# Attention and two-matrix MoE on one core: twelve chunks of GELU on VectorE, and last units of two chunks

## The chip, the core and the metric

The kernel runs on one core of a Trainium2 chip. The metric is the device time of one execution in microseconds (us). The core has a matmul engine (TensorE, PE in the profile; its weight loads are PEld), a vector engine (VectorE, DVE), an engine for activation functions (ScalarE, ACT), GpSimd (POOL) and SyncE (SP), which here only issues DMAs. Each engine works through its own instructions in order and waits for others by semaphores.

## What is computed

```python
kv_pool = kv.reshape(B, H // 4, 4, W // 4, 4, C).mean(axis=(2, 4))
k = v = kv_pool.reshape(B, -1, C) @ w_sr          # 768 keys of 128 per batch
s = (q @ k.transpose(0, 2, 1)) / np.sqrt(C)       # softmax over the keys
x = (softmax(s) @ v).reshape(B * N, C)            # 49152 rows of 128
h = x @ w_in                                      # 128 -> 2048
out = (h / (1 + np.exp(-1.702 * h))) @ w_out      # 2048 -> 128
```

B is 4, N 12288, C 128. The last line is a GELU in its sigmoid form.

## The kernel before

**Tiles and stages.** The rows are cut into 96 groups of 512. For a group the attention has 6 chunks (128 keys x 512 rows of scores, one exponential each) and the MoE 16 chunks (128 of the 2048 hidden columns x 512 rows, one GELU each). There are two rounds of 48 groups: attention, MoE, attention, MoE. The second MoE, groups 48 to 95, is the last stage.

**Units.** ScalarE takes mostly three chunks at a time, a unit of 128x1536 from three banks of PSUM; units alternate between banks 0 to 2 and 3 to 5. TensorE fills a unit with three matmuls (`fill_attn`, L330; `fill_moe`, L513), ScalarE writes exp or GELU of it to a frame of `ag` in SBUF (L332, L515), and TensorE drains each chunk later: four matmuls of 128x129 with v for attention (L341), one of 128x512 with w_out for the MoE (`drain_moe`, L523). A group's 16 drains sum up in one accumulator bank, 6 or 7; then VectorE transposes it out of PSUM (L531) and SP issues four DMAs to the output. Groups use the two banks in turn. The very last group is drained in small matmuls of 128x128 (`drain_last`, L544) into banks 2, 5, 6 and 7, the one that the group before still holds last; VectorE and ScalarE copy the result out, half each.

**Chunks of exponentials on VectorE.** 32 attention chunks do not go through ScalarE: 24 of four "early" groups and 8 "rolling" ones (`early_fill`, `early_exp`). TensorE makes their scores in one of the two accumulator banks (L373); VectorE reads them there in its first step (L389) and then computes 2 to the power of z by splitting off the integer part as exponent bits (L391 to L395) and a polynomial of degree five (L397, L400, L402). The steps are dealt out one by one between VectorE's other work. The rolling ones are kept in `aside`, three places of their own.

**What sets the order.** The order on every engine is fixed when the program is written, by a planner at the end of the kernel. Its clock counts in matmuls of 512 columns. It holds estimates of when TensorE (`now`), VectorE (`dve`) and each unit of ScalarE (`end`) will be done, with

```python
FIXED, CHUNK, SWITCH, HANDOVER, EVACUATE = 0.295, 1.978, 6.0, 1.0, 4.5
end.append(begin + FIXED + CHUNK * len(part))
limit = end[-1] - K - HANDOVER if n + 3 < len(seq) else 1e9
```

For each unit n it places the fills of unit n + 2, and then drains as long as they end before `limit`, so that the next fills are in time for ScalarE. A unit of three counts 6.229 of these units on ScalarE, and three fills and three drains count 6 on TensorE, so that now and then a fourth drain fits. Chunks that ScalarE has made and TensorE has not drained wait in `ag` (102 places); they are the backlog. `seq` is the list of units. In the second MoE it is 250 units of three, then `rest`: eight of two and two of one.

Of the kernel before, what the change touches and what calls it, by code (L numbers as in the profile page):

```python
# [7 lines left out]
F32 = mybir.dt.float32  # L8
F32R = mybir.dt.float32r
I32 = mybir.dt.int32  # L10
BF = mybir.dt.bfloat16
AF = mybir.ActivationFunctionType
AX = mybir.AxisListType
ADD = mybir.AluOpType.add
MUL = mybir.AluOpType.mult
GE = mybir.AluOpType.is_ge
LE = mybir.AluOpType.is_le
SUB = mybir.AluOpType.subtract
MAX = mybir.AluOpType.max
MIN = mybir.AluOpType.min  # L20
# [4 lines left out]
def kernel(  # L25
    ctx, tc, q, kv, w_sr, moe_w_in, moe_w_out, out,
):
    nc = tc.nc
# [7 lines left out]
    FCH = d_ff // 128  # L36
    scale = 1.0 / (C ** 0.5)
    G = 512
    SG = 4 * G
# [4 lines left out]
    K = 3  # L44
# [14 lines left out]
    R = 2  # L59
    XS = NS // R  # L60
# [8 lines left out]
    qpool = ctx.enter_context(tc.tile_pool(name="qpool", bufs=4))  # L69
    agpool = ctx.enter_context(tc.tile_pool(name="ag", bufs=1))  # L70
    npool = ctx.enter_context(tc.tile_pool(name="norm", bufs=3))
# [12 lines left out]
    def acc(key=None):  # L84

        nonlocal last_acc
        last_acc = next_acc()
        if key:
            closes[last_acc] = key
        return banks[:, last_acc, :]  # L90
# [13 lines left out]
    x = xpool.tile([128, XS * SG], BF, name="x")  # L104
# [160 lines left out]
    for m in range(0, 128, 32):  # L265
        p = slice(m, m + 32)
# [16 lines left out]
    w_in_sb = cpool.tile([128, d_ff], BF)  # L283
# [28 lines left out]

    early = range(NG // R, NG // R + EARLY)
    rolling = [(i, JC - 1) for i in [*range(38, NG // R, 6), *range(57, 90, 6)]]
    aside = agpool.tile([128, K, 512], BF, name="aside")

    def weights(c):
        if c[0] == "a" and c[1] in early:
            return ag[:, (c[1] - early[0]) * JC + c[2], :]
        if c[0] == "a" and c[1:] in rolling:  # L320
            return aside[:, rolling.index(c[1:]) % K, :]
        return ag[:, slot_of[c], :]


# [42 lines left out]
    COEFFS = (1.0000001192092896, -0.6931469440460205, 0.24022120237350464, -0.05550713464617729, 0.009675541892647743, -0.001327647129073739)  # L367

    def early_fill(i, jc):
        nonlocal steps  # L370
        ps = acc()
        rhs = qTs[i // 4][:, 0, (i % 4) * G:(i % 4 + 1) * G]
        nc.tensor.matmul(ps, kTs[i // GB][:, jc * 128:(jc + 1) * 128], rhs, start=True, stop=True)  # L373
        steps = early_exp(ps, weights(("a", i, jc)))
        early_step()

    def early_step():
        nonlocal steps
        on_dve(next(steps))
        if steps.gi_frame.f_locals["last"]:  # L380
            steps = None
            made[early_todo.pop(0)] = dve

    def early_exp(ps, out):
# [18 lines left out]
        last = True  # L403
        yield 3.5

    made, used = {}, []
    steps, early_todo = None, [c for c in rolling if c[0] < early[0]]
    early_todo += [(i, jc) for i in early for jc in range(JC)]
    early_todo += [c for c in rolling if c[0] > early[-1]]

    def early_fits(p, i, jc):
        if (i, jc) in rolling:
            group = seq[p][1][0][0] if seq[p][0] == "a" else seq[p][1][0][0] // (NG // R) * (NG // R) + NG // R - 1
            return (i // GB, jc) in vs and i // 4 - 1 <= group // 4 and len(used) > rolling.index((i, jc)) - K
        return low and min(slot_of.values()) >= low and (2, JC - 1) in vs

    def early_waits(t):
        return any(made.get((t // 4, jc), 1e9 if (t // 4, jc) in early_todo else 0.0) > now for jc in range(JC))
# [98 lines left out]
    def drain_moe(g, fc):  # L517
        if fc == 0:
            o_of[g] = acc(("o", g))
        if g == NG - 1:  # L520
            drain_last(g, fc)
            return
        nc.tensor.matmul(o_of[g], w_out_sb[:, fc, :], weights(("m", g, fc)),  # L523
                         start=(fc == 0), stop=(fc == FCH - 1))
        del slot_of["m", g, fc]
        if fc == FCH - 1:
            close(("o", g), max(now, dve - 1.0) + EVACUATE)
            on_dve(3.6)

            o_sb = opool.tile([128, 512], F32, name="o_sb")  # L530
            nc.vector.transpose(o_sb, o_of.pop(g))  # L531
            for m in range(4):
                nc.sync.dma_start(out=out_r[g, m],
                                  in_=o_sb[32 * m:32 * m + 32, :].rearrange("i (b j) -> i b j", j=32))
# [33 lines left out]
    for n in range(R):  # L568
        part = [c for c in chunks if c[0] // (NG // R) == n]
        while part:  # L570
            m = sizes.pop(0) if sizes else K
            seq.append(("a", part[:m]))
            part = part[m:]
        todo += [("a", t, a) for t in range(n * NT // R, (n + 1) * NT // R) for a in range(2)
                 if (t // TS * TS + TS - 1) // 4 not in early]
        flat = [(g, fc) for g in range(n * NG // R, (n + 1) * NG // R) for fc in range(FCH)]
        todo += [("m",) + c for c in flat]
        rest = [2] * 8 + [1, 1] if n == R - 1 else []
        while flat:
            m = K if len(flat) > sum(rest) else rest.pop(0)  # L580
            seq.append(("m", flat[:m]))
            flat = flat[m:]
# [7 lines left out]
            at["a", i, jc] = at["a", early[-1] + 1, 0] - 1  # L590
    for i, jc in rolling:
        at["a", i, jc] = at["a", i, 0]
    for kind, t, a in [k for k in todo + todo_early if k[0] == "a"]:
        at["at", t, a] = max(at["a", t // 4, jc] for jc in range(a * K, a * K + K))

# [5 lines left out]
    def prepare(p):  # L601
# [10 lines left out]
        for i, jc in part:  # L612
# [36 lines left out]
            transpose_q: (1.05, 4.2), early_fill: (1.0, 5.5), key_and_value: (0.55, 3.5),  # L649
            transpose_pooled: (0.9, 3.6), make_k: (0.8, 3.2), make_v: (0.8, 3.7)}  # L650
    SMALL = 0.26
    PAUSE = 4.0
    now, end, extra_at = 0.0, [], 0.0
    source, dve = None, 0.0
# [25 lines left out]
    for n in range(len(seq)):  # L680
        fill(n + 2)
        while True:
            room = room_ahead()
            limit = end[-1] - K - HANDOVER if n + 3 < len(seq) else 1e9
            bank = free[next_acc()]
            f = None
            if extras and now >= max(extra_at, bank):
                f, *args = extras[0]
            if steps and dve <= now + 2.0:
                early_step()  # L690
            if not f and not steps and early_todo and early_fits(min(n + 2, len(seq) - 1), *early_todo[0]) and dve <= now + 2.0 and now >= bank:
                f, args = early_fill, early_todo[0]
            if f and max(now, bank) + COST[f][0] > limit + (0.0 if f is early_fill else 4.5) and room >= 4 * K:
                f = None
            if f:
                now = max(now, bank) + COST[f][0]
                f(*args)
                free[last_acc] = dve + 1.0 if f is early_fill else now + COST[f][1]
                if f in (transpose_pooled, make_k, make_v):
                    on_dve(2.5)  # L700
                extra_at = max(now + PAUSE, dve + 1.5 if f in (transpose_pooled, make_k, make_v) else 0.0)
                if f is early_fill:
                    pass
                else:
                    extras.pop(0)
                continue
            if not source:

                if todo_early and not any(early_waits(t) for t in range(todo_early[0][1], todo_early[0][1] + TS)):
                    source = todo_early  # L710
                else:
                    source = todo
            if not source:
                break
            kind, i, c = source[0]
            needs = at[("at" if kind == "a" else kind, i, c)]
            cost = K * SMALL if kind == "a" else 1.0
            first_of = c == 0 and (kind == "m" or i % TS == 0)
            if source is not todo_early and (needs > n or (kind == "a" and first_of and at["at", i + TS - 1, 1] > n)
                                             or (kind == "a" and (early_waits(i) or first_of and early_waits(i + TS - 1)))):  # L720
                if first_of:
                    source = None
                break
            start = now if source is todo_early else max(now, end[needs] + HANDOVER)
            if first_of:
                start = max(start, bank)
            if start + cost > limit and not (room < 2 * K + 1 or (room < 4 * K and start == now)):
                if first_of:
                    source = None
                break  # L730
            now = start + cost
            (drain_attn if kind == "a" else drain_moe)(i, c)
            source.pop(0)
            if kind == "a" and i // 4 in early:
                early_left -= 1
                if not early_left:
                    low = 0
            if c == (1 if kind == "a" else FCH - 1) and (kind == "m" or i % TS == TS - 1):
                source = None
# [31 lines left out]
```

## Time and profile before

| what | value |
|---|---|
| median of 4 runs | 956.94 us (956.66 to 956.95) |
| the profiled execution | 956.94 us, its span 955.2 us |
| granted TensorE clock | 1.000 |
| PE, ACT, DVE, PEld busy | 943.1, 940.2, 383.4, 503.8 us |
| first fill of the second MoE | 603.55 us |
| last activation ends | 950.4 us |
| last matmul starts, copies to SBUF | 950.9 us, 951.1 to 951.6 us |
| VectorE busy in 652 to 702 us | 5.7 of 50 us |

The profile is one execution. The span runs from the first to the last instruction; what lies around it is 1.7 us. Busy times of PE and ACT contain overlap of an instruction with the one in front of it, so a share near 100% says that the engine had something in hand, and not that it ran at its best rate. PEld counts the weight loads, one ahead of each matmul, at 98 ns.

### The profile page before, as it was taken

To read this page: it belongs to the slowest core of one execution; us is meant where nothing else is said; L and a number is where in the kernel's file an instruction comes from. 1 tells how busy PE (TensorE), PEld (TensorE's weight loads), DVE (VectorE), ACT (ScalarE), POOL (GpSimd) and SP (SyncE) were. 2 spreads that over 40 slices of the span, in tenths; PEclk is the share of its full clock that TensorE was granted. 3 is DMA by queue.
4 is the path that set the end of the run, shared out by engine and by line. 5 is a ranking of instruction groups with operands and counts; after the bars stand their busy time and mean duration, and the time that the engine had idled before them with its cause. 6 is when DMAs were issued, how large, how long until landed. Compare 5 with 4: busy or idle time off the path is not lost.

```text
span 955.2 us, 15289 instructions
## 1 busy us (share of the span) xinstructions
PE 943.1 (99%) x6330; PEld 503.8 (53%) x6330; DVE 383.4 (40%) x822; ACT 940.2 (98%) x708; POOL 68.0 (7%) x118
## 2 busy tenths in 40 slices
PE   7899999999999999999999999999999999999998
PEld 3677777444444444454446777754444444444444
DVE  5443663111677777787545774411010111101010
ACT  5999999999999999999999999999999999999998
POOL 4100101320000332000000000000000000000000
PEclk9999999999999999999999999999999999999999
DMA  9989993999752898215268984562222222222222
GB/s 182 201 165 173 187 211 52 152 139 174 158 118 39 115 149 108 39 28 84 34 103 150 177 158 87 133 117 38 45 37 41 42 36 45 34 45 37 41 34 45
DMA packets 371237, 94.39 MB, mean 99 GB/s; under 512 B 344608, under 2 KB 368800, under 8 KB 370848
## 3 DMA queue, kind: packets, MB, share of 16 engines
q1 hardware_dynamic: 341728, 60.78, 37.1%
q0 software_dynamic: 29168, 32.51, 22.2%
q8 instruction: 49, 0.80, 0.4%
q14 instruction: 20, 0.16, 0.1%
q10 hardware_dynamic: 272, 0.13, 0.0%
HBM read 52.49 MB, written 48.23 MB: 105 GB/s over the span
## 4 chain that ended last, share of the span: by engine, by line
ACT 86%; PE 12%; DMA 1%; issue 0%; DVE 0%; POOL 0%; POOLq 0%
ACT ag L515 72%; ACT ag L332 14%; PE banks L341 6%; PE banks L330 5%; DMA x<-in_kv_dram 1%; PE banks L134 0%; DVE x L355 0%; PE banks L228 0%; PE banks L544 0%; ACT L515 0%; ACT L332 0%; POOL x L217 0%; PE banks L513 0%; PE banks L280 0%; DVE qT L234 0%
## 5 line engine op out<-in xcount | busy, mean ns | idle before, releaser
L515 ACT ACTIVATE ag<-banks 128x1536 bf16<-128x1536 f32 (+1 forms) x516 | 688.7, 1513 | 0.0
L513 PE MATMUL banks<-x,w_in_sb 128*128 128x512 bf16 x1536 | 415.6, 379 | 0.4 <-ACT ag L515 0.3
L523 PE MATMUL banks<-ag,w_out_sb 128*128 128x512 bf16 x1520 | 408.9, 379 | 0.0
L332 ACT ACTIVATE ag<-banks 128x1536 bf16<-128x1536 f32 (+2 forms) x186 | 245.4, 1470 | 3.7 <-PE banks L330 3.6
L523 PEld LDWEIGHTS <-w_out_sb 128*128 128x128 bf16 x1520 | 148.5, 98 | 178.3
L513 PEld LDWEIGHTS <-w_in_sb 128*128 128x128 bf16 x1536 | 148.0, 98 | 170.7 <-issue 7.5
L531 DVE STREAM_TRANSPOSE o_sb<-banks 128x512 f32<-128x512 f32 x95 | 68.1, 716 | 373.7 <-PE banks L523 360.0
L341 PEld LDWEIGHTS <-ag 128*128 128x128 bf16 x2272 | 145.3, 98 | 43.7 <-issue 1.1
L341 PE MATMUL banks<-v,ag 128*128 128x129 bf16 x2272 | 162.6, 220 | 0.2
L330 PE MATMUL banks<-qT,kT 128*128 128x512 bf16 x544 | 147.7, 379 | 3.9 <-ACT ag L332 2.2
L400 DVE SCALAR_TENSOR_TENSOR ea<-ea,eb 128x512 f32<-128x512 f32 x128 | 87.9, 687 | 3.9 <-DVE ea L400 0.8
L355 DVE TENSOR_TENSOR x<-banks,rec 128x384 bf16<-128x384 f32 x128 | 71.3, 557 | 4.4
L352 DVE RECIPROCAL rec<-banks 128x3 f32<-128x3 f32 x128 | 22.9, 179 | 102.3 <-PE banks L341 102.0
L330 PEld LDWEIGHTS <-kT 128*128 128x128 bf16 x544 | 46.7, 98 | 30.3 <-issue 3.7
L168 POOL DMA_DIRECT2D kvs<-in_kv_dram x32 | 40.3, 1319 | 25.4 <-DMA kvs<-in_kv_dram 22.8
L389 DVE TENSOR_SCALAR ea<-banks 128x512 f32<-128x512 f32 x32 | 22.1, 692 | 33.7 <-PE banks L373 33.7
L444 POOL MEMSET gate_tile<- 1x1 f32 x39 | 3.5, 88 | 432.8 <-DVE gate_tile L443 432.7
L395 DVE SCALAR_TENSOR_TENSOR eb<-eb,ea 128x512 f32<-128x512 f32 x32 | 22.0, 687 | 0.8
L402 DVE SCALAR_TENSOR_TENSOR ag<-ea,ee 128x512 bf16<-128x512 f32 x24 | 16.5, 689 | 1.1
L397 DVE TENSOR_SCALAR ea<-eb 128x512 f32<-128x512 f32 x32 | 13.9, 434 | 0.8
L393 DVE TENSOR_SCALAR ee<-eb 128x512 int32<-128x512 f32 x32 | 13.7, 429 | 0.9
L391 DVE TENSOR_SCALAR eb<-ea 128x512 f32<-128x512 f32 x32 | 13.6, 425 | 1.0
(66 smaller groups left out, 154.6 us busy)
## 6 DMA issues: line engine op xcount, KB each, us to landing
out_dram<-o_sb SPq DMA_DIRECT2D x380, 64.0 KB, 2.0
x_bf<-x SPq DMA_DIRECT2D x16, 768.0 KB, 6.0
kvs<-in_kv_dram POOLq DMA_DIRECT2D x32, 384.0 KB, 6.3
q_bf<-in_q_dram POOLq DMA_DIRECT2D x20, 512.0 KB, 7.5
x<-in_kv_dram POOLq DMA_DIRECT2D x12, 512.0 KB, 10.7
x<-in_q_dram POOLq DMA_DIRECT2D x7, 256.0 KB, 15.3
w_in_sb<-in_moe_w_in_dram POOLq DMA_DIRECT2D x1, 512.0 KB, 6.8
w_out_sb<-in_moe_w_out_dram POOLq DMA_DIRECT2D x1, 512.0 KB, 10.4
```

The costliest lines, as they stand in the source:

```text
L168: nc.gpsimd.dma_start(out=kv_sums[b][:, i2], in_=kv_p[b, i, w, :, i2], **({"accum_op": ADD} if n else {}))
L330: nc.tensor.matmul(ps[:, k, :], kTs[i // GB][:, jc * 128:(jc + 1) * 128], rhs, start=True, stop=True)
L332: nc.scalar.activation(place([("a",) + c for c in chunks]), ps, AF.Exp, scale=scale)
L341: nc.tensor.matmul(av_of[u][:, k * (C + 1):(k + 1) * (C + 1)], weights(("a", i, jc))[:, o:o + T], vs[i // GB][:, jc, 0:C + 1], start=(jc = ...
L352: nc.vector.reciprocal(rec, ps[:, :, C])
L355: nc.vector.tensor_tensor(to, ps[:, :, 0:C], rec.unsqueeze(2).broadcast_to([128, TS, C]), MUL)
L389: nc.vector.tensor_scalar(a, ps, scale / LN2, -126.0, MUL, MAX)
L400: nc.vector.scalar_tensor_tensor(a, a, COEFFS[k], b, ADD, MUL)
L513: nc.tensor.matmul(ps[:, k, :], w_in_sb[:, fc * 128:(fc + 1) * 128], x[:, g % (4 * XS) * G:(g % (4 * XS) + 1) * G], start=True, stop=True)
L515: nc.scalar.activation(place([("m",) + c for c in chunks]), ps, AF.Gelu_apprx_sigmoid)
L523: nc.tensor.matmul(o_of[g], w_out_sb[:, fc, :], weights(("m", g, fc)), start=(fc == 0), stop=(fc == FCH - 1))
L531: nc.vector.transpose(o_sb, o_of.pop(g))
```

## The change

Twelve more chunks are taken from ScalarE: the last of the 16 chunks of groups 52, 55, 58 to 85 in the second MoE (`lent`). TensorE makes such a chunk by `early_fill`, in an accumulator bank, up to two groups ahead of its place. VectorE copies it times -1.702/ln 2 into a buffer `raw` (a tile of q's pool), computes 2 to that power as before, adds 1, takes the reciprocal in two halves of 256 columns, and multiplies by `raw` and a constant into `aside`. The drain reads it from there. The list of units no longer contains these chunks, and its end is nine units of two. The planner gets a cost for the reciprocal (10.5 of its units) and does not begin to drain a group whose lent chunk is planned to be made later.

```diff
+    lent = [(g, FCH - 1) for g in range(52, 88, 3)]
...
+        if c[0] == "m" and c[1:] in lent:
+            return aside[:, (len(rolling) + lent.index(c[1:])) % K, :]
         return ag[:, slot_of[c], :]
...
     def early_fill(i, jc):
-        nonlocal steps
+        nonlocal steps, raw
         ps = acc()
+        if (i, jc) in lent:
+            if raw is None:
+                raw = qpool.tile([128, 1, SG], BF, name="qT")[:, 0, 0:2 * G].bitcast(F32)
+            nc.tensor.matmul(ps, w_in_sb[:, jc * 128:(jc + 1) * 128],
+                             x[:, i % (4 * XS) * G:(i % (4 * XS) + 1) * G], start=True, stop=True)
+            steps = lent_gelu(ps, weights(("m", i, jc)))
+            early_step()
+            return
...
+    def lent_gelu(ps, out):
+        last = False
+        a = npool.tile([128, 512], F32, name="ea", bufs=1)
+        b = npool.tile([128, 512], F32, name="eb", bufs=1)
+        e = npool.tile([128, 512], I32, name="ee", bufs=1)
+        nc.vector.tensor_scalar_mul(raw, ps, -1.702 / LN2)
+        yield 3.5
+        nc.vector.tensor_scalar(a, raw, -126.0, 127.0, MAX, MIN)
+        yield 2.2
+        nc.vector.tensor_scalar_add(b, a, MAGIC)
+        yield 2.2
+        nc.vector.tensor_scalar(e, b, MAGIC - 127.0, 2.0 ** 23, SUB, MUL)
+        yield 2.2
+        nc.vector.scalar_tensor_tensor(b, b, MAGIC, a, SUB, SUB)
+        yield 3.5
+        nc.vector.tensor_scalar_mul(a, b, COEFFS[5])
+        yield 2.2
+        for k in (4, 3, 2, 1):
+            nc.vector.scalar_tensor_tensor(a, a, COEFFS[k], b, ADD, MUL)
+            yield 3.5
+        nc.vector.scalar_tensor_tensor(a, a, COEFFS[0], e.bitcast(F32), ADD, MUL)
+        yield 3.5
+        nc.vector.tensor_scalar_add(a, a, 1.0)
+        yield 2.2
+        for m in (0, 256):
+            nc.vector.reciprocal(b[:, m:m + 256], a[:, m:m + 256])
+            yield RECIPROCAL
+        nc.vector.scalar_tensor_tensor(out, raw, -LN2 / 1.702, b, MUL, MUL)
+        last = True
+        yield 3.5
+
+    raw = None
...
-    early_todo += [c for c in rolling if c[0] > early[-1]]
+    early_todo += [c for c in rolling if c[0] > early[-1]] + lent
...
+        if (i, jc) in lent:
+            return seq[p][0] == "m" and seq[p][1][0][0] >= i - 2 and len(used) > len(rolling) + lent.index((i, jc)) - K
...
-        del slot_of["m", g, fc]
+        if (g, fc) in lent:
+            used.append((g, fc))
+        else:
+            del slot_of["m", g, fc]
...
-        rest = [2] * 8 + [1, 1] if n == R - 1 else []
+        flat = [c for c in flat if c not in lent]
+        rest = [2] * 9 if n == R - 1 else []
...
+    for g, fc in lent:
+        at["m", g, fc] = at["m", g, 0]
...
+    RECIPROCAL = 10.5
...
             if source is not todo_early and (needs > n or (kind == "a" and first_of and at["at", i + TS - 1, 1] > n)
+                                             or (kind == "m" and first_of and (i, FCH - 1) in lent
+                                                 and made.get((i, FCH - 1), 1e9) > now + 1.0)
```

## The prediction, on record before the result

> **What bounds the kernel now.** I read the page's busy line first, then its groups. ScalarE (ACT) and TensorE (PE) both look full, and the chain of the end is given to ScalarE's activations, so a chunk taken from ScalarE seems to be a sure gain.
>
> ```profile
> PE 943.1 (99%) x6330; PEld 503.8 (53%) x6330; DVE 383.4 (40%) x822; ACT 940.2 (98%) x708; POOL 68.0 (7%) x118
> ...
> ACT 86%; PE 12%; DMA 1%; issue 0%; DVE 0%; POOL 0%; POOLq 0%
> ...
> L515 ACT ACTIVATE ag<-banks 128x1536 bf16<-128x1536 f32 (+1 forms) x516 | 688.7, 1513 | 0.0
> L513 PE MATMUL banks<-x,w_in_sb 128*128 128x512 bf16 x1536 | 415.6, 379 | 0.4 <-ACT ag L515 0.3
> ```
>
> Both engines overlap an instruction with the one before (1513 ns for an activation that comes every 1.34 us, 379 ns for a matmul that comes every 0.216 us), so neither busy share can tell which of the two waits. The weight loads can: one load goes with each matmul. The next view is the busy time by stretches of the second MoE (its first fill is at 603.55 us). The columns after the length are PE, PEld, DVE, ACT and POOL busy with their counts.
>
> ```profile
> 652.00:702.00 50.00, 50.00 (x234) 22.65 (x232) 5.73 (x8) 50.00 (x38) 0.00 (x0) 1.00 0.24 38
> ...
> 852.00:883.00 31.00, 31.00 (x145) 14.06 (x144) 3.58 (x5) 31.00 (x25) 0.00 (x0) 1.00 0.24 37
> 883.00:903.00 20.00, 20.00 (x92) 8.83 (x91) 2.15 (x3) 20.00 (x16) 0.00 (x0) 1.00 0.24 36
> 903.00:923.00 20.00, 20.00 (x91) 8.61 (x89) 1.44 (x2) 20.00 (x17) 0.00 (x0) 1.00 0.26 41
> 923.00:940.00 17.00, 17.00 (x77) 7.36 (x76) 2.15 (x3) 17.00 (x14) 0.00 (x0) 1.00 0.23 35
> ```
>
> From 652 to 883 us there are 1070 loads in 231 us, one per 0.2158 us, and PEld stands at 45.3%. After 903 it falls to 43%. The timeline of PE's loads says the same: a steady row at 850 us, and at 927 us a hole in front of each fill.
>
> ```profile
> 850.01 0.53 PEld L523 LDWEIGHTS <-w_out_sb 128*128 128x128 bf16 x3
> 850.66 0.53 PEld L513 LDWEIGHTS <-w_in_sb 128*128 128x128 bf16 x3
> 851.30 0.75 PEld L523 LDWEIGHTS <-w_out_sb 128*128 128x128 bf16 x4
> ...
> 927.32 0.31 PEld L513 LDWEIGHTS <-w_in_sb 128*128 128x128 bf16 x2 [0.17 <-issue]
> 927.75 0.53 PEld L523 LDWEIGHTS <-w_out_sb 128*128 128x128 bf16 x3
> ```
>
> So **TensorE is the bound of the second MoE up to about 883 us**, and ScalarE only of its last 65 us. The reason lies in the order of the matmuls: TensorE enters the MoE about 50 chunks behind (made, not yet multiplied by w_out), works this off with an occasional fourth drain in a unit, and only with six chunks left does it wait for ScalarE.
>
> The Trainium skill, "Perfetto Trace Analysis", section "Identifying the Most-Contended Engine", says to improve first the engine with the highest occupancy, and to judge TensorE by LDWEIGHTS busy share and not by matmul busy. By its first half ScalarE at 98% would be the one to relieve, and the gain would be ScalarE's whole saving. The trace supports the second half, with a caution: here 45.3% of loads is already a TensorE without a hole.
>
> **What TensorE can still give.** From the first fill (603.55) to the end of the last matmul (24 of L544 from 949.64, one per 0.0557 us, so 950.98) are 347.43 us. The work in it: 768 fills and 752 drains at 0.2158, 228 attention drains at 0.0561 (12 of L341 in 0.84 us less one latency of 0.22), 64 small matmuls of the last group at 0.0557: 328.0 + 12.8 + 3.6 = 344.36 us. TensorE idles 3.07 us in all. The change adds and removes no matmul, so **3.07 us is the most that it can bring**, whatever ScalarE saves.
>
> **The change, part by part.**
>
> *ScalarE.* 756 chunks instead of 768: 246 activations of three and 9 of two, instead of 250, 8 of two and 2 of one. A unit of three takes 1.344 us, of two 0.917, of one 0.485 (spacing of the fills at the end). 4 x 1.344 + 2 x 0.485 - 0.917 = **5.43 us** less. Until 883 us it lies beside TensorE's work and is worth nothing by itself.
>
> *The order on TensorE.* It is identical up to the first fill of the second MoE. After it the planner, which believes ScalarE to be the slower, hands out fewer fourth drains per group, since ScalarE now asks for the fills sooner. Counted from the changed order, the backlog is 50 chunks at the 20th unit in both, but 22 instead of 5 at the last fill. These 22 are worked off after ScalarE is done: behind the last two fills stand 8 drains of the last but one group and all 64 small matmuls. Before, only 24 small ones stood there. So what ScalarE gives is taken back at the end, up to the idle time of TensorE that really goes.
>
> *Idle time that stays or comes.* (a) 0.1 us at the entry, as before. (b) The nine units of two: TensorE needs 4 x 0.2158 = 0.863 us for one, ScalarE 0.917, and the step from units of three to units of two leaves a hole (0.27 us before). With what lead TensorE has then, I count 0.5 to 0.8 us, and take 0.8. (c) The last group. Nine of its small matmuls follow the last drain of the group before (0.216 + 0.5 us after that began), then come those in the bank that this group still holds. VectorE's transpose starts 0.41 us after the last drain began (944.36 to 944.77 in the tail's timeline), takes 0.716 (L531) and the hand-over some 0.05: 1.18 - 0.716 = 0.47 us. Before, two fills and more small ones lay between. (d) One lent fill stands between the end of a group and the first drain of the next, which then needs the bank just closed: 3 fills, the lent one and the last drain are 1.08 us against 1.18: 0.1 us. Sum 0.1 + 0.8 + 0.47 + 0.1 = 1.47 us against 3.07: **1.6 us gained**.
>
> *VectorE.* A lent chunk is 1 pass from PSUM (L389, 0.692; with its gap 0.72), 5 of one tensor (L391, L393, L397: 0.43; 0.46), 7 of two tensors (L395, L400: 0.687; 0.72) and 2 reciprocals of 128x256: 8.1 us + 2r. The trace has a reciprocal of 128x3 only (L352, 179 ns). From below r is 0.18 us, if its time is all fixed; from above 256/3 x 0.179 = 15.3 us, if none is. I take 2.27, the plan's own 10.5 units at 0.216, which also is nearer to the fixed end, where a pass of 512 columns takes 0.69. Then a lent chunk is 12.6 us, with three transposes 14.8, of the 20.7 us in which three groups pass; VectorE is 10% busy there now. It comes 34 to 40 us ahead of its drain (158 to 188 matmuls at 0.2158), so it is hidden, and up to r = 5.2 us the answer is the same. At the upper end VectorE would need 41 us every 20.7 and lose over 200.
>
> The Trainium skill, "VectorE: DVE Perf Modes", section "Walkthrough: the 8-slice pipeline in each mode", has the reciprocal divide with a repeat count of 8; an estimate from that page is 256 x 8 / 0.96 GHz = 2.1 us, no row here shows it, and the sum would be the same by it.
>
> *Waits added.* Each lent fill needs one of two accumulator banks for 0.42 + 0.69 us. On VectorE the pass that frees it stands behind nothing but finished work, and transposes queued behind a reciprocal come at most 2.3 us late for a bank that is needed 6.7 us later. In the first MoE the same path runs for the early exponentials: in the waits of 240 to 420 us, with 19 of them, PE has no entry at all. No DMA and nothing on SP's or POOL's queues moves past another; the bank of raw values lies in a buffer of q that nobody reads any more.
>
> **Sum.** The profiled execution: span 955.2, time 956.94, which is the median. 956.94 - 1.6 = **955.3 us** (-0.17%). About 0.2%, 1.9 us, is what a measurement of this kernel can tell from no change.
>
> **Rivals.**
> - *The idle time goes further* (17%): TensorE's lead covers the units of two, and the last transpose is earlier; 2.0 to 3.0 us gained, 954.5. For it: the fills of 652 to 883 us run without any hole at the same pace. Against it: the 0.47 us of the last transpose has no cover in the order.
> - *ScalarE bounds after all* (5%): the gain is 5.43, 951.5. For it: 98% busy and 86% of the chain. Against it: the loads.
> - *Bank waits* (12%), the slow side: TensorE has no slack, so each wait for VectorE counts in full. If every lent chunk holds up a bank by one pass (0.69 us), 12 x 0.69 = 8.3 us, and the time is 956.94 - 1.6 + 8.3 = 963.6. From 0.13 us per chunk nothing is gained; from 0.29 it is slower by over 0.2%. For it: by the counts of (d) four of the twelve hand-overs have under 0.15 us to spare. Against it: the early exponentials cause none.
> - *Small bank waits* (8%): 0.05 to 0.2 us per chunk, 955.9 to 957.7.
>
> That the change does not do what it says is excluded by the order: ScalarE's queue has 255 activations in the second MoE, VectorE's 12 chains.
>
> **How the numbers follow.** Forecast 58%, 955.0 to 955.6. Faster by over 0.2%: 17 + 5 = 22%. Within: 58 + 8 = 66%. Slower: 12%. The range takes in the first and last rivals: 954.0 to 957.7; ScalarE's case and the large waits are left out (17%).
>
> **What would show it.** Right: PEld at 45% until the last fill; ScalarE's last activation 5 to 5.5 us before its old place, but the last matmul only 1.6; over 60 L544-like matmuls in one row at the end; about 0.5 us of PE waiting for the last but one transpose. Wrong: a list of PE waiting for VectorE at the lent fills, or holes in the loads in the middle of the MoE. A reciprocal far above 5 us would void it all.

## The result, and the profile after

The changed kernel takes **955.26 us** (median of 39 runs, 955.00 to 957.22) against 956.82 before (59 runs). The ratio is 0.9984, 95% interval 0.9980 to 0.9989: about 1.6 us less. The profiled execution took 955.39 us with a span of 953.6, at a granted clock of 1.000.

The page's busy line of the changed kernel, and its row of the 128x256 reciprocal, which the kernel before does not have:

```profile
PE 941.9 (99%) x6330; PEld 504.0 (53%) x6330; DVE 512.7 (54%) x1002; ACT 934.8 (98%) x703; POOL 68.3 (7%) x118
...
L442 DVE RECIPROCAL eb<-ea 128x256 f32<-128x256 f32 x24 | 40.8, 1725 | 0.4
```

ScalarE's busy time is 5.4 us less (940.2 to 934.8), just what was taken from it. The kernel is only 1.6 us shorter. VectorE has 129 us more, and TensorE waits for it only once, for a transpose at the very end (below). The next view has the busy time by stretches of the changed kernel; the columns are PE, PEld, DVE, ACT and POOL, each with its count.

```profile
652.00:702.00 50.00, 50.00 (x233) 22.67 (x232) 29.97 (x40) 50.00 (x38) 0.00 (x0) 1.00 0.24 37
...
883.00:903.00 20.00, 20.00 (x94) 9.11 (x93) 2.15 (x3) 20.00 (x16) 0.00 (x0) 1.00 0.27 42
903.00:923.00 20.00, 20.00 (x95) 9.07 (x93) 2.15 (x3) 20.00 (x16) 0.00 (x0) 1.00 0.26 40
923.00:940.00 17.00, 16.94 (x79) 7.49 (x78) 1.77 (x3) 17.00 (x15) 0.00 (x0) 1.00 0.22 34
940.00:950.00 10.00, 9.23 (x89) 5.87 (x87) 1.52 (x3) 5.34 (x7) 0.00 (x0) 1.00 0.34 52
```

PEld keeps its 45% past 883 us now: 93 loads in 20 us, where 91 and 89 were before. TensorE is full up to the units of two. In the last row ScalarE is busy for 5.3 of 10 us, and TensorE goes on without it. The tail's timeline (start, duration, engine, line) shows what it goes on with:

```profile
942.27 0.59 PE L558 MATMUL banks<-x,w_in_sb 128*128 128x512 bf16 x2
...
943.18 0.59 PE L558 MATMUL banks<-x,w_in_sb 128*128 128x512 bf16 x2
...
943.61 1.89 PE L568 MATMUL banks<-ag,w_out_sb 128*128 128x512 bf16 x8
...
945.34 0.67 PE L592 MATMUL banks<-w_out_sb,ag 128*128 128x128 bf16 x9
...
945.54 0.72 DVE L579 STREAM_TRANSPOSE o_sb<-banks 128x512 f32<-128x512 f32 x1 [5.16 <-PE banks L568]
946.31 3.23 PE L592 MATMUL banks<-w_out_sb,ag 128*128 128x128 bf16 x55 [0.30 <-DVE o_sb L579]
```

The fills of the units of two come every 0.92 us, while four matmuls need 0.863: a hole of 0.056 us in each. The last fills are at 943.18; behind them stand 8 drains and all 64 small matmuls, 5.3 us of work (8 x 0.2158 + 64 x 0.0557). Nine small matmuls end near 945.84, and the other 55 begin at 946.31, when the transpose is done: TensorE waits 0.47 us.

### The profile page after: what moved, and what is told of

Same layout as the page of the kernel before. It is cut to its first block, busy times and chain, and to the rows that moved or that the text cites. A ratio compares the mean times of both kernels' runs of the same rounds, so it can differ in the third digit from the quotient of the medians.

```text
span 953.6 us, 15432 instructions
## 1 busy us (share of the span) xinstructions
PE 941.9 (99%) x6330; PEld 504.0 (53%) x6330; DVE 512.7 (54%) x1002; ACT 934.8 (98%) x703; POOL 68.3 (7%) x118
## 4 chain that ended last, share of the span: by engine, by line
ACT 84%; PE 12%; DMA 2%; issue 1%; DVE 0%; SPq 0%; POOLq 0%
ACT ag L560 71%; ACT ag L335 13%; PE banks L344 6%; PE banks L333 5%; DMA x<-in_kv_dram 2%; PE banks L568 0%; PE banks L558 0%; PE banks L134 0%; DMA out_dram<-o_sb 0%; DVE x L358 0%; SPq L581 0%; ACT L560 0%; ACT L335 0%; PE banks L228 0%; DVE o_sb L579 0%
## 5 line engine op out<-in xcount | busy, mean ns | idle before, releaser
L411 DVE SCALAR_TENSOR_TENSOR ea<-ea,eb 128x512 f32<-128x512 f32 x128 | 87.9, 687 | 4.0 <-DVE ea L411 0.8
L442 DVE RECIPROCAL eb<-ea 128x256 f32<-128x256 f32 x24 | 40.8, 1725 | 0.4
L435 DVE SCALAR_TENSOR_TENSOR ea<-ea,eb 128x512 f32<-128x512 f32 x48 | 33.0, 688 | 1.4
L422 DVE TENSOR_SCALAR qT<-banks 128x512 f32<-128x512 f32 x12 | 8.3, 692 | 31.3 <-PE banks L378 31.1
```

Source lines behind the costliest of these rows:

```text
L411: nc.vector.scalar_tensor_tensor(a, a, COEFFS[k], b, ADD, MUL)
L435: nc.vector.scalar_tensor_tensor(a, a, COEFFS[k], b, ADD, MUL)
L442: nc.vector.reciprocal(b[:, m:m + 256], a[:, m:m + 256])
```

## The experiments

Theory: **TensorE bounds the second MoE up to about 883 us**, and what the change can bring is TensorE's idle time, 3.07 us from the first fill to the end of the last matmul. Rival 1: ScalarE bounds it, and its saving of 5.4 us was lost at the hand-overs to VectorE. Rival 2: VectorE's part costs something at each lent chunk. The times are medians of 4 to 11 runs of each kernel, and more of the first two. The median of the kernel before was 956.7 to 956.8 us beside every one.

| kernel | us | ratio to before, 95% interval | TensorE idle in its second MoE, us |
|---|---|---|---|
| before | 956.82 | | 3.06 |
| the change | 955.26 | 0.9984 (0.9980 to 0.9989) | 1.39 |
| early activations narrower | 956.74 | 0.9999 (0.9990 to 1.0008) | 3.06 |
| late activations narrower | 954.72 | 0.9978 (0.9969 to 0.9987) | 1.0 |
| last units alone | 956.59 | 0.9999 (0.9990 to 1.0008) | 2.9 |
| six lent chunks | 954.53 | 0.9976 (0.9967 to 0.9985) | 0.8 |
| reciprocal twice | 955.15 | 0.9982 (0.9973 to 0.9991) | 1.40 |
| held bank later | 954.76 | 0.9978 (0.9970 to 0.9987) | 0.93 |
| held bank later, units of three | 953.63 | 0.9966 (0.9954 to 0.9979) | 0.36 |
| eighteen lent chunks | 969.83 | 1.0136 (1.0121 to 1.0152) | 16.3 |
| before, 24 fills twice | 961.98 | 1.0054 (1.0040 to 1.0068) | 3.06 |
| change, 24 fills twice | 960.40 | 1.0037 (1.0023 to 1.0051) | 1.40 |
| lent chunks alone | 955.61 | 0.9987 (0.9978 to 0.9996) | 1.9 |
| eighteen, lower price | 956.89 | 1.0003 (0.9993 to 1.0012) | 3.4 |

The last column is the time from the first fill of the second MoE to the end of the last matmul in the trace, less the matmuls in it at 0.2158, 0.0561 and 0.0557 us (344.37 us, and 5.18 more where 24 fills are made twice). It is of the one profiled execution, so it can differ from the medians by a few tenths.

### ScalarE's work taken away, early and late

```diff
+    cut = set()
...
-        nc.scalar.activation(place([("m",) + c for c in chunks]), ps, AF.Gelu_apprx_sigmoid)
+        wide = place([("m",) + c for c in chunks])
+        if chunks[0][0] in range(52, 88, 3) and chunks[0][0] not in cut and len(chunks) == K and chunks[0][1] > 2:
+            cut.add(chunks[0][0])
+            wide, ps = wide[:, 0:2, :], ps[:, 0:2, :]
+        nc.scalar.activation(wide, ps, AF.Gelu_apprx_sigmoid)
```

> The kernel before, with twelve activations of the second MoE (one in each of groups 52, 55, 58 to 85) made over two chunks instead of three; the third chunk's GELU is left out and its drain multiplies what its place held. ScalarE is spared 12 x 0.427 = 5.1 us at the very groups of the change; TensorE's matmuls, their order and VectorE stay as before. Theory (TensorE bounds the second MoE up to 883 us): no change, 956.8 within 0.3. Rival 1 (ScalarE bounds it, and the change lost its saving to waits at the hand-over to VectorE): 5.1 less, 951.7.

The second kernel has `range(84, 96)` in its place.

> The same cut in groups 84 to 94 (eleven activations, 4.7 us of ScalarE), nine of them after 883 us, where TensorE's loads show holes. Theory: here ScalarE bounds, and the holes in front of the fills close, 48 x 0.051 = 2.4 us less what the units of two at the end keep: 1.5 to 2.0 us less, 955.0. Rival 1: 4.7 less, 952.1, the same per activation as in the early groups.

Early: 956.74, no change. Late: 954.72, 2.1 us less. In the early kernel ScalarE is busy less and the loads stay what they were. First the row of the kernel before:

```profile
652.00:883.00 231.00, 231.00 (x1072) 104.70 (x1070) 25.09 (x35) 231.00 (x173) 0.00 (x0) 1.00 0.26 40
```

Then two rows of the early kernel:

```profile
652.00:883.00 231.00, 229.89 (x1051) 104.73 (x1071) 25.11 (x35) 228.21 (x173) 0.00 (x0) 1.00 0.26 40
...
903.00:923.00 20.00, 19.95 (x90) 8.63 (x90) 1.50 (x3) 20.00 (x16) 0.00 (x0) 1.00 0.26 40
```

ACT is busy 228.2 of 231 us there, and 1071 loads take the same 231 us as before. (Some matmul records are missing from this trace, 1051 against 1072, so its PE column is a little low; the loads are all there.) In the late kernel the loads of the end go up to 93 in 20 us:

```profile
903.00:923.00 20.00, 19.89 (x93) 9.06 (x93) 2.15 (x3) 19.81 (x17) 0.00 (x0) 1.00 0.25 38
```

The same 0.43 us of ScalarE per activation is worth nothing at the groups of the change and about 0.2 us each at the end. More was not to be had there: the trace of the kernel before has 38 holes of about 0.05 us in front of fills, from 891 to 940 us, 1.9 us in all (the expectation counted 48), and eight of the eleven activations lie behind 883 us, not nine. Rival 1 falls: neither kernel has a hand-over to VectorE, and the early saving is lost all the same.

### TensorE's work added

```diff
-            nc.tensor.matmul(ps[:, k, :], w_in_sb[:, fc * 128:(fc + 1) * 128],
-                             x[:, g % (4 * XS) * G:(g % (4 * XS) + 1) * G], start=True, stop=True)
+            for _ in range(2 if 54 <= g < 78 and fc == 7 else 1):
+                nc.tensor.matmul(ps[:, k, :], w_in_sb[:, fc * 128:(fc + 1) * 128],
+                                 x[:, g % (4 * XS) * G:(g % (4 * XS) + 1) * G], start=True, stop=True)
```

> The kernel before with one fill of each of groups 54 to 77 made twice (the second writes the same again): 24 matmuls of 512 columns, 5.18 us, more on TensorE; ScalarE and VectorE have the same work. Theory (TensorE is full there, and ScalarE is made to wait for it): 5.2 more, 962.0. Rival 1 (ScalarE bounds, and TensorE has 1.344 - 6 x 0.2158 = 0.05 us to spare in each of 128 units): hidden, 956.8 to 957.5.

> The changed kernel with the same 24 fills made twice. Theory: 5.2 more than the changed kernel, 960.4. Rival 1: as far as the saving of ScalarE has made TensorE the bound, the part over ScalarE's old time: at most 2, 957.

961.98 and 960.40: 5.1 us more on either kernel for 5.18 us of matmuls. TensorE has nothing to spare in these groups, before the change as after it. This is the strongest evidence for the theory, since it needs no counting of holes. The kernel before with the added fills, in the same stretch as above:

```profile
652.00:883.00 231.00, 231.00 (x1072) 104.72 (x1071) 24.39 (x34) 229.51 (x169) 0.00 (x0) 1.00 0.25 39
```

TensorE makes as many loads in the 231 us as before, 24 of them for the added fills, and ScalarE gets 169 activations done in place of 173.

But ScalarE had hardly anything to spare either. In the kernel before, the ends of its activations in this stretch are 1.3445 us apart on average, and 1.3433 from 895 to 938 us, where TensorE waits for it: 0.2 us of waiting in 171 activations. So both engines run at their best pace here, and the backlog makes that possible, since a fourth drain now and then takes up what TensorE would have over. Work taken from ScalarE alone then gains nothing, because TensorE is full; work added to ScalarE alone should cost nearly its full time, but no run here adds any.

### The number of lent chunks

```diff
-    lent = [(g, FCH - 1) for g in range(52, 88, 3)]
+    lent = [(g, FCH - 1) for g in range(52, 88, 6)]
```

> The changed kernel with six lent chunks instead of twelve (every sixth group from 52 on). Theory: the gain does not follow the number of chunks, since TensorE's idle time is what can be had; six chunks leave a backlog of 9 instead of 22 at the last fill, and fills stand between the last transpose and the matmuls that need its bank, so that the hole of 0.47 us goes: 954.6 to 954.9, a little faster than twelve. Rival 1 (the saving of ScalarE, less a fixed price per chunk at the hand-over): half the gain of the change, 956.0.

954.53: half the chunks bring 2.3 us, more than twelve bring. ScalarE's saving is then 2.7 us, and the backlog at the last fill is 9, so that fills stand between the last transpose and the matmuls that need its bank.

```diff
+    lent = [(g, FCH - 1) for g in range(52, 88, 2)]
```

> The changed kernel with eighteen lent chunks, in every second group. ScalarE is spared 2.6 us more. VectorE then has 11.5 us for the chain and 1.4 for two transposes in 13.8 us, and the plan, which counts 2.27 us for a reciprocal, thinks that it falls behind and holds groups back until their chunk is made: the backlog rises to 83 chunks at the last fill instead of 22. Theory: TensorE waits for the fills meanwhile and has 60 more drains (13 us) at the end: 967 to 969. Rival 1: 2.6 us less than the changed kernel, 952.7.

969.83, a little over the expected range. Behind the last fill its trace has 68 drains and the 64 small matmuls, which is a backlog of 82 chunks and the two that the last fills make. The waits of this kernel from 604 to 960 us, longest first in total (waiter, then what it waited for: us, times, longest):

```profile
DVE o_sb L579 <- PE banks L568: 60.8, 39, 8.0
DVE qT L422 <- PE banks L378: 35.3, 18, 2.7
PEld L558 <- issue: 18.8, 27, 0.8
PE banks L558 <- ACT ag L560: 11.2, 23, 0.5
```

TensorE does not wait for VectorE in this stretch (it does once after it, 0.47 us for the last transpose, as in the changed kernel). It stands in front of fills whose banks ScalarE still reads, because the plan gave it no drains in the meantime. And VectorE waits 35 us for lent fills, so it is not full. That pointed to the plan's price of a reciprocal.

```diff
-    RECIPROCAL = 10.5
+    RECIPROCAL = 8.0
```

> The kernel with eighteen lent chunks (969.8), its plan told 8.0 for a reciprocal in place of 10.5, which is what the chip took (1.725 us at 0.2158). The instructions are the same, only their order is planned anew; the backlog at the last fill falls from 83 to 44 chunks, and fewer units go by without drains. Theory a (VectorE had time, the plan held TensorE's groups back for a price that is too high): 956.8 to 957.5, 12 us less, and still not faster than twelve chunks. Theory b (VectorE is full with eighteen chunks): about 969 as before, with TensorE waiting for VectorE at the lent drains.

956.89: 13 us less for the same instructions in another order. Theory a holds. Eighteen chunks still gain nothing: TensorE is idle for 3.4 us, about as long as before the change. Of these, 1.4 us are in two units near 890 us that still go without drains, 0.27 just ahead of them, 0.65 at the units of two and 0.47 at the last transpose.

### VectorE's work doubled

```diff
             nc.vector.reciprocal(b[:, m:m + 256], a[:, m:m + 256])
+            nc.vector.reciprocal(b[:, m:m + 256], a[:, m:m + 256])
```

> The changed kernel with each reciprocal made twice: VectorE has 2 x 1.7 us more for a lent chunk, the order of every engine stays. Theory: VectorE's chain comes 34 to 40 us ahead of its drain and has 20.7 us; with 15 us for the chain and 2.1 for three transposes it is still hidden: no change, 955.3 within 0.2. Rival 2 (VectorE's part costs TensorE something at each lent chunk, through transposes and banks that come late): 12 x 0.3 to 12 x 1.7 us more, 959 or above.

955.15, against 955.26: 41 us more on VectorE cost nothing. Rival 2 falls.

### The end of the kernel

> The kernel before with the last units of the change alone: nine units of two in place of eight of two and two of one; no chunk on VectorE. Theory: the wait of 0.48 us in front of the last fill goes (a unit of one was too short to hide it), the rest stays: 0.5 us less, 956.3. Rival 1 (only ScalarE's time counts): ScalarE saves 2 x 0.485 - 0.917 = 0.05 us, and four more small matmuls stand behind the last activation: 0.2 us more, 957.0.

956.59: 0.2 us less by the medians where 0.5 was expected, and its interval does not tell that from no change. The hole in front of the last fill went as expected, but eight small matmuls instead of four wait for the last activation, a wait that the theory's sum left out (the rival names it). The last 28 small matmuls in the trace:

```profile
948.63 2.03 PE L544 MATMUL banks<-w_out_sb,ag 128*128 128x128 bf16 x28
```

They take 2.03 us, where 27 spacings of 0.0557 and a latency of 0.22 make 1.72.

> The changed kernel with the old last units (eight of two and two of one): the twelve lent chunks alone. Theory: before the last fills a unit of one is too short to hide TensorE's wait for its bank, 0.4 to 0.5 us more than the changed kernel, 955.7. Rival (the parts add up: the change brought 1.6, the last units alone 0.2): 955.5.

955.61, between the two, so it does not decide between them. The median lies 0.35 us above the changed kernel, and TensorE's idle time in the traces 0.5 us. By the medians the lent chunks alone bring 1.2 us, the last units alone 0.2, and both together 1.6.

```diff
-        parts = [(m, fc) for m in range(4) if m != held or fc > 2]
-        if fc == 2:
-            parts += [(held, f) for f in range(3)]
+        parts = [(m, fc) for m in range(4) if m != held or fc > 7]
+        if fc == 7:
+            parts += [(held, f) for f in range(8)]
...
```

> The changed kernel, where the last group's small matmuls in the bank that the group before still holds begin after eight chunks of the other banks instead of three. Theory: the one wait of TensorE for VectorE at the end, 0.47 us, is covered by 15 more small matmuls (0.83 us): 954.8. Rival 1 (TensorE's holes do not count, ScalarE's work does): no change, 955.3.

954.76: 0.5 us less for the 0.47 us of waiting, and 0.46 us less idle time in the trace. With it, the last kernel has no units of two:

```diff
-        rest = [2] * 9 if n == R - 1 else []
+        rest = []
```

> As the run before, and the second MoE's units are of three chunks to the end (no units of two). Theory: the holes of the units of two (0.22 + 7 x 0.056 = 0.6 us) go too; what is left of TensorE's idle time is 0.2 us at the entry and one hand-over, and perhaps 0.1 to 0.4 us where the last small matmuls need a bank that the last activation still reads: 954.1 to 954.5, faster than both kernels. Rival 1: ScalarE's work is 0.25 us less and its last unit 0.4 us longer: 955.4.

**953.63**, faster than both kernels, and 0.5 us below the expected range. Its tail (timeline of PE):

```profile
942.09 0.81 PE L558 MATMUL banks<-x,w_in_sb 128*128 128x512 bf16 x3
942.73 1.89 PE L568 MATMUL banks<-ag,w_out_sb 128*128 128x512 bf16 x8
944.46 3.76 PE L592 MATMUL banks<-w_out_sb,ag 128*128 128x128 bf16 x64
```

Fills, drains and small matmuls follow without a hole. TensorE is idle for 0.36 us in the whole second MoE, 2.7 us less than before. The profiled executions, 956.94 and 953.63, differ by 3.3 us: 0.2 of the rest is an earlier start of the second MoE (603.33 against 603.55), and 0.4 a shorter end, 3.8 instead of 4.2 us from the last matmul to the last instruction. Both lie outside what the theory counts, and that is why the time fell below the expected range. Why the end is shorter here is open.

## Why the prediction was right

The forecast was 955.3 us; the time was 955.26. The mechanism was right. That the number agrees to 0.04 us is partly luck: one term was 0.18 us too large and another 0.05 too small, and the forecast started from 956.94, the median of 4 runs, where that of 59 is 956.82. Point by point:

- **TensorE bounds, ScalarE only the last 65 us.** Shown for what a saving of ScalarE is worth, by the narrower activations (0 early, 2.1 us late) and by the added fills (5.1 for 5.18). Two things are less sharp than the prediction has them: the first hole in front of a fill comes at 891 us, not 883, and up to there ScalarE is at its own pace too (1.3445 us for a unit of three, against 1.3433 where it bounds).
- **3.07 us is the most that can be had.** The best kernel leaves 0.36 of it; its time fell by slightly more than 3.07, by what lies outside the second MoE's matmuls, which the prediction took as fixed. For the change itself the trace shows 1.39 us of idle time where the sum had 1.47.
- **The entry:** 0.15 us up to 625 us, against 0.1 (0.13 in the kernel before).
- **Units of two:** 0.224 + 7 x 0.056 = 0.62 us against 0.8, which I had taken at the upper end. This is the one term that was mis-sized by more than 0.1.
- **The held bank** (the wait for the last transpose): 0.467 us against 0.47; taking it away gave 0.5.
- **The hand-over between a group's end and the next first drain:** 0.106 us against 0.1, at 662 us, and at no other lent chunk more than 0.04.
- **The backlog:** 22 chunks at the last fill, as the order had them; ScalarE's last activation ended at 945.0 instead of 950.4 us, the last matmul 1.6 us earlier. The loads stayed at 45% up to 923 us; from there to 940, with the units of two, they were at 44% (7.49 of 17 us), where the prediction had 45% to the last fill.
- **The reciprocal:** 1.725 us against the 2.27 taken between 0.18 and 15.3. It is off, but below the 5.2 us at which it would have counted, and doubling it changed nothing. The Trainium skill, "VectorE: DVE Perf Modes", section "Walkthrough: the 8-slice pipeline in each mode", has a repeat count of 8. My estimate of 2.1 us from it is nearer, but also too high: the row gives at most 1.725/256 us = 6.7 ns per column, 6.5 cycles of 0.96 GHz.
- **ScalarE's 5.43 us:** the busy time fell by 5.4. It was right as a size and, as the working said, not the gain. The Trainium skill, "Perfetto Trace Analysis", section "Identifying the Most-Contended Engine", names the engine of highest occupancy first and judges TensorE's headroom by its LDWEIGHTS share. Here the share, 45.3%, was no sign of headroom: it was a full TensorE, as the added fills confirm. What decided was that the row of loads had no hole.

The rivals: the idle time did go further in the kernels with fewer lent chunks or another end (954.76 to 953.63), but not in the change. Bank waits did not occur but for the counted one. The chances placed faster by over 0.2% at 22%, and the measured 0.16% lies just inside the bound.

## What to carry to other kernels

Where two engines are both shown as busy all the time, count the items of each per us (here weight loads, and the ends of activations) and compare with the best spacing that the trace has. An engine at its best spacing is full, whatever its busy share says, and both can be: then a saving on one is worth only the holes of the other. With a backlog, a saving on the engine that makes the work only moves the backlog to the end, so look at what stands behind the last fill before working on the middle. And where a planner decides the order, a price in it that is too high can cost more than the work itself: 13 us for half a microsecond per reciprocal.

## What was not expected of the hardware

A reciprocal of 128x256 took 1.725 us, one of 128x3 (from PSUM) 0.18, so that nearly all of it seems to go with the columns: some 6 ns each (1.546 us for 253 columns more), against 1.34 ns (687/512) at most for a pass of two tensors. Run beside TensorE and ScalarE, 41 us more of it did not lengthen the kernel (955.15 against 955.26), and TensorE's idle time stayed at 1.40 us. Left open: why the kernel's part ahead of the second MoE ends between 603.2 and 603.8 us in the profiles, though its matmuls are the same and in the same order in all of them.
